# Strassen's seven products for Gate and Up of the last two token tiles in place of Down's

## The chip, the cores and the metric

One core of a Trainium2 chip runs the whole kernel. The metric is the device time of one execution in microseconds (us). The kernel before takes 804.02 us (median of 3 timed runs, 803.73 to 804.4). Engines are named as in the profile: PE (TensorE matmuls), PEld (its weight loads), DVE (VectorE), ACT (ScalarE), POOL (GpSimd), SP (the queue that issues most DMAs).

## What is computed

A layer norm of x (2048 tokens, 512 features) feeds two branches. One is sliding-window attention with 32 heads of 16 features and a window of 256, followed by a 512x512 projection; the other is a gated feed-forward with 1792 hidden features. The output is x + attention * silu(feed-forward).

```python
xn = _layernorm(x, axis=-1)
s = attention(xn, A_wqkv, A_wo)          # 32 heads of 16, window 256
gate = xn @ w1                            # 512 -> 1792
up = xn @ w3                              # 512 -> 1792
g = silu((silu(gate) * up) @ w2)          # 1792 -> 512
return x + s * g
```

Everything is float32 at the edges. Inside, each float32 operand is held as a float16 high part and a float16 low part, so that a product is three matmuls (high*high, low*high, high*low). All matmul weights are scaled by powers of two first.

## The kernel before

**Tiles.** The tokens stand in four tiles `t` of 512 (`NT`, `TW`). The hidden features stand in 14 blocks `f` of 128 (`FB`). For one `t` and `f`, `gate_up` (L1048) makes two pieces of 12 matmuls of 512 columns: Gate, then Up, each into a PSUM bank of its own (`bank`, L163, which hands out `m0` and `m1` in turn; there are only these two). ACT takes the tanh of Gate (L1074), DVE multiplies it with Gate (L1078) and with Up (L1083), and the result is split into a high and a low half for Down.

**Down** adds up the 14 blocks. For tiles 0 and 1, `down` (L1272) does it in four groups of blocks and four blocks of tokens: 336 matmuls of 512 columns (L1284). For tiles 2 and 3 Strassen's algorithm is used: `fold_weights` (L998) makes sums of w2's quarters once, during tile 1, and stores them in `dFold`; `fold_first` and `fold_second` (L1119, L1131) make the sums of the hidden activations on POOL; `fold_down_piece` (L1186) runs the seven products, 588 matmuls of 256 columns (L1202); ACT and DVE read them out (L1216, L1220), and `unfold` (L1226) adds the seven results to four blocks of output.

**Attention** is cut into 32 units (a tile, a group of 8 heads, half of it). In each unit `pass1` (L653) finds the row maxima of the next scores (PE L671, DVE L685) and `pass2` (L738) makes scores (PE L759), masks (DVE L766), exponentials (ACT L769) and the products with V (PE L787). The scores have two PSUM tiles of two banks (`pss`), the products with V one (`pso`).

**What sets the order.** PE's order is the order of the program text. A unit's attention comes in four or five batches; `spread` (L1508) puts pieces of dense work (Gate, Up, Down, projections, values, totals) between them by their cost in columns. `later(n, f)` (L144) puts work n steps on. For the other engines a scheduler chooses the order when the program is built, and then each engine runs its own list from front to back. Work that reads a PSUM bank is put forward there (`urgent`, L138). Slots in SBUF come from `take` and `give` (L113, L120).

**Ends.** `total` (L1316) multiplies the attention by `wo` and joins the branches. After the last attention unit the queue runs off what is left: in the kernel before the last Gate and Up, the last seven Down products, `unfold`, and the four totals.

Of the kernel before, what the change touches and what calls it, by code (L numbers as in the profile page):

```python
# [10 lines left out]
F32 = mybir.dt.float32  # L11
# [28 lines left out]
XS = 2.0**10  # L40
# [4 lines left out]
HS = 2.0**4  # L45
# [7 lines left out]
SLOTS = 54  # L53
ORDERED = {ENGINE.PE}
GROUPS = ((0, 4), (4, 8), (8, 11), (11, 14))
FOLDS = ((0, 4), (4, 7))
FOLD_AT = (0, 1, 3, 5, 7, 9, 11)
# [26 lines left out]
def tile_block(ctx: ExitStack, tc: tile.TileContext, x, wqkv, wo, w1, w3, w2, out):  # L84
# [17 lines left out]
    fpool = pool("fpool", 2)  # L102
    psm = pool("psm", 1, PSUM)
# [57 lines left out]
    open_bank = [0]  # L161

    def bank(shape, dtype=F32):  # L163

        open_bank[0] = b = 1 - open_bank[0]
        return psm.tile(shape, dtype, name=f"m{b}", tag=f"m{b}", bufs=1)
# [62 lines left out]
    dFold = dram.tile([len(KINDS), P, FB // 2, 2 * D], F16, name="dFold")  # L229
# [117 lines left out]

    WQ = {}
# [3 lines left out]
    def weights(name, w):  # L352
# [16 lines left out]
        def cut(apart=0):  # L369
            if name == "wo":  # L370

                made = [take(F16) for _ in range(NC)]
                hi, lo = ([m[:, k * D:(k + 1) * D] for m in made] for k in range(2))
            else:
                both = [const.tile([P, NC, D], F16, name=f"{name}{k}") for k in "hl"]
                hi, lo = ([b[:, c, :] for c in range(NC)] for b in both)
# [176 lines left out]
    def value(j, scores_bank=False):  # L553
# [4 lines left out]
        def part(half):  # L558
# [9 lines left out]
            if half:  # L568
                with urgent():
                    nc.scalar.activation(V[:, j % VB, 0:H * VW].rearrange("p (h w) -> p h w", w=VW)[:, :, 0:DH],  # L570
                                         pv.rearrange("p (h d) -> p h d", d=DH), AF.Copy, scale=sc["uv"])
        return opening([(6, lambda h=h: part(h)) for h in range(2)])
# [294 lines left out]
    sg_scale = const.tile([P, FB], F32, name="sgs")  # L867
    p13 = const.tile([P, FB], F32, name="p13")
# [16 lines left out]
    def measure(f, apart=0, until=8):  # L885
# [4 lines left out]
        def scale(s=None):  # L890
            pp = small.tile([P, 2, 2], F32, name="pp")
            pi = small.tile([P, 2, 2], F32, name="pi")
# [3 lines left out]
        def rest(pp, pi):  # L896
# [5 lines left out]
            def cut(i, k):  # L902
# [3 lines left out]
                split_pool(a[:, 0:D], a[:, D:], raws[i][k], pi[:, k, i:i + 1])  # L906
# [18 lines left out]
    def load_down(t, f):  # L925
        if t:
            WF[t, f][1] = b = take(F16)
# [5 lines left out]
    def measure_down(k, f):  # L933
# [21 lines left out]
        def rest(p2):  # L955
# [5 lines left out]
            if k:  # L961
                nc.vector.tensor_max(fold_q, fold_q, q)
            else:
                nc.vector.tensor_copy(fold_q, q)
# [16 lines left out]
            if f1 == FB:  # L981
                later(4, fold_scales)
        beside_scores(2, scale)

    fold_q = const.tile([P, 1], F32, name="fq")
    fold_down = const.tile([P, 1], F32, name="fd")
    fold_w = const.tile([P, FB], F32, name="fw")
    folded = []

    def fold_scales():  # L990

        folded.append(0)
        with tc.issue_after(lasts["emptied"].ins):
            nc.vector.tensor_scalar(fold_down, fold_q, 1.0 / (HS * WS), None, op0=ALU.mult)
            nc.vector.reciprocal(fold_q, fold_q)
            nc.vector.tensor_scalar(fold_w, p13, fold_q, WS, op0=ALU.mult, op1=ALU.mult)

    def fold_weights(j):  # L998

        cell = {}  # L1000
        l, r = slice(0, 256), slice(256, 512)
        sub = nc.gpsimd.tensor_sub

        def load():
            cell["raw"] = [take(F32) for _ in range(2)]
            for i, raw in enumerate(cell["raw"]):
                lasts["load"] = nc.sync.dma_start(raw, w2[(2 * j + i) * P:(2 * j + i + 1) * P, :])

        def sums():
            assert folded  # L1010
            e, o = cell["raw"]
            for i, raw in enumerate((e, o)):
                with behind_exp():
                    nc.scalar.activation(raw, raw, AF.Copy, scale=fold_w[:, 2 * j + i:2 * j + i + 1])
            cell["z"] = z, y = [take(F32) for _ in range(2)]
            sub(z[:, l], e[:, r], e[:, l])
            sub(z[:, r], o[:, r], z[:, l])
# [686 lines left out]
```

## Time and profile before

| what | value |
|---|---|
| median of 3 timed runs | 804.02 us (803.73 to 804.4) |
| span of the profiled execution, first to last instruction | 801.8 us |
| granted PE clock, mean | 1.000 |
| DVE busy | 623.0 us, 78% of the span |
| ACT busy, POOL busy | 393.9 us, 381.2 us |
| DMA engines' mean share, q1 | 55.4% |
| HBM read, written | 91.23 MB, 36.57 MB |

The profile has no other time of its own execution than the span; the timed runs lie 2.2 us above it, for what comes before the first and after the last instruction. A row of a group reads: line, engine, operation, tile written <- tiles read, shapes, count | busy us, mean ns of one | idle time ahead of it and whom it waited for. A row of the timeline reads: start, length, engine, line, operation, count. A row of the table by stage reads: stage, its length, then the busy time (and number of instructions) of PE, PEld, DVE, ACT and POOL, PE's granted clock, the DMA share and GB/s.

### The profile page before, as it was taken

The numbers are of one execution on the slowest core, as the hardware profiler recorded it, in microseconds if no ns is written. First come the engines' busy times: TensorE is split into PE (matmuls) and PEld (weight loads), VectorE is DVE, ScalarE is ACT, GpSimd is POOL, SyncE is SP. The second block draws the span as 40 slices with busy tenths as digits, with TensorE's granted clock in tenths as the row PEclk, the third lists the DMA queues.
The fourth block names the chain that finished last, engine by engine and source line by source line (L and its number), as shares of the span: only waits on it lengthen the run. The fifth ranks groups of instructions, "written<-read, shape, count | busy, mean of one in ns | idle before, by whom it ended". The sixth has DMA issues, their size and how long they took to land.

```text
span 801.8 us, 23974 instructions
## 1 busy us (share of the span) xinstructions
PE 791.1 (99%) x9181; PEld 403.8 (50%) x9181; DVE 623.0 (78%) x2005; ACT 393.9 (49%) x592; POOL 381.2 (48%) x746
## 2 busy tenths in 40 slices
PE   8999999999999999999999999999999999999997
PEld 4443445444454444444445444466544744466465
DVE  8887889778797778787888887776678876874537
ACT  6989777744355544344443344344434334444411
POOL 2355657633229435365442546330446276650770
PEclk9999999999999999999999999999999999999999
DMA  9987654636666565657555733665453553334431
GB/s 281 245 258 238 196 185 144 248 111 208 173 215 189 169 210 144 214 148 258 130 194 173 213 114 101 177 173 157 137 159 87 159 157 110 89 117 134 129 94 56
DMA packets 109858, 134.18 MB, mean 167 GB/s; under 512 B 18928, under 2 KB 64944, under 8 KB 109744
## 3 DMA queue, kind: packets, MB, share of 16 engines
q1 hardware_dynamic: 109456, 132.13, 55.4%
q8 instruction: 72, 1.18, 0.6%
q10 hardware_dynamic: 288, 0.52, 0.2%
q14 instruction: 42, 0.34, 0.1%
HBM read 91.23 MB, written 36.57 MB: 159 GB/s over the span
## 4 chain that ended last, share of the span: by engine, by line
PE 80%; DVE 8%; DMA 4%; ACT 3%; issue 2%; POOL 1%; SPq 1%; DVEq 0%; ACTq 0%; POOLq 0%
PE m L1059 31%; PE po L787 9%; PE m L601 8%; PE m L1202 8%; PE m L1284 7%; PE s L759 5%; PE m L1336 4%; PE m L567 4%; PE s L671 3%; DMA slot<-in_B_w_dram 2%; DVE junk L685 2%; PE po L671 2%; ACT sqa L249 1%; DVE s L766 1%; POOL slot L345 1%
## 5 line engine op out<-in xcount | busy, mean ns | idle before, releaser
L1059 PE MATMUL m<-XH,slot 128*128 128x512 f16 x896 | 267.3, 380 | 1.1 <-DVE slot L1078 0.6
L769 ACT ACTIVATE pt<-s,es 128x1024 f32<-128x1024 f32 x152 | 167.6, 1112 | 178.7 <-DVE s L766 176.9
L1059 PEld LDWEIGHTS <-slot 128*128 128x128 f16 x1344 | 124.9, 98 | 155.6 <-issue 13.1
L1059 PE MATMUL m<-XL,slot 128*128 128x512 f16 x448 | 169.8, 379 | 0.0
L766 DVE TENSOR_TENSOR s<-s,MK 128x256 f32<-128x256 f32 (+2 forms) x280 | 118.7, 434 | 53.5 <-PE s L759 49.8
L685 DVE CUSTOM_DVE_ANT_0 junk<-s,MW 128x320 bf16<-128x320 f32 x276 | 133.9, 485 | 18.4 <-PE s L671 11.4
L339 POOL TENSOR_TENSOR slot<-slot,slot 128x256 f16<-128x256 f32 (+1 forms) x86 | 57.6, 692 | 128.8 <-ACT slot L1092 60.0
L345 POOL TENSOR_TENSOR slot<-slot,slot 128x128 f16<-128x128 f32 x168 | 68.9, 444 | 76.6 <-ACT slot L343 76.6
L685 DVE CUSTOM_DVE_ANT_0 junk<-po,MW 128x320 bf16<-128x320 f32 x172 | 83.4, 485 | 4.6
L1284 PE MATMUL m<-slot,slot 128*128 128x512 f16 x336 | 78.5, 380 | 1.1 <-DVE slot L1078 1.1
L787 PE MATMUL po<-pt,V 64*32 64x320 f32 (+4 forms) x2880 | 77.2, 342 | 0.1
L601 PE MATMUL m<-XH,slot 128*128 128x512 f16 x240 | 70.8, 380 | 0.5 <-DVE slot L1078 0.5
L1202 PE MATMUL m<-slot,slot 128*128 128x256 f16 x588 | 68.4, 273 | 0.0
L1074 ACT ACTIVATE slot<-m,sgs 128x512 f32<-128x512 f32 x56 | 38.3, 684 | 59.8 <-PE m L1059 59.7
L1117 POOL TENSOR_TENSOR slot<-slot,slot 128x256 f16<-128x256 f32 x98 | 64.6, 671 | 1.1
L1202 PEld LDWEIGHTS <-slot 128*128 128x128 f16 x588 | 56.2, 98 | 11.5 <-issue 2.8
L787 PEld LDWEIGHTS po<-pt,V 64*32 64x32 f32 x2880 | 50.4, 106 | 22.4 <-issue 0.8
L1078 DVE SCALAR_TENSOR_TENSOR slot<-slot,m 128x512 f32<-128x512 f32 x56 | 38.3, 684 | 28.9 <-ACT slot L1074 26.7
L759 PE MATMUL s<-qa,KA 50*64 50x320 f16 (+3 forms) x1472 | 58.3, 259 | 0.0
L601 PEld LDWEIGHTS <-slot 128*128 128x128 f16 x392 | 36.5, 98 | 42.6 <-issue 1.7
L759 PEld LDWEIGHTS <-KA 50*64 50x64 f16 x1472 | 30.1, 105 | 51.7 <-issue 32.8
L1284 PEld LDWEIGHTS <-slot 128*128 128x128 f16 x336 | 30.7, 98 | 39.2 <-issue 4.7
(194 smaller groups left out, 1131.5 us busy)
## 6 DMA issues: line engine op xcount, KB each, us to landing
slot<-dW SPq DMA_DIRECT2D x98, 256.0 KB
slot<-in_B_w_dram SPq DMA_DIRECT2D x56, 256.0 KB
slot<-dFold SPq DMA_DIRECT2D x48, 256.0 KB
dW<-slot SPq DMA_DIRECT2D x42, 256.0 KB
slot<-in_A_x_dram SPq DMA_DIRECT2D x30, 256.0 KB
KA<-dK SPq DMA_DIRECT2D x24, 288.0 KB
slot<-dWQ SPq DMA_DIRECT2D x24, 256.0 KB
qa<-dQ SPq DMA_DIRECT2D x30, 192.0 KB
```

Of the source, the lines that this page charges most:

```text
L339: op(out[:, c], a[:, c], b[:, c])
L345: nc.gpsimd.tensor_sub(lo[:, c:c + P], raw[:, c:c + P], hi[:, c:c + P])
L601: nc.tensor.matmul(cell["pp"][:, cols[n]], w[:, (a * NC + c) * P:(a * NC + c + 1) * P], b[:, c, cols[n]], start=n == 0 and (c, i) == parts ...
L685: lasts["maximum"] = nc.vector.tensor_tensor_reduce(out=junk[:, :n], in0=s[:, r, :n], in1=mask, scale=1.0, scalar=NEG, op0=ALU.add, op1=AL ...
L759: nc.tensor.matmul(s[64 * h:64 * h + 64, r, o:o + 64 * n], ka[rows, 2 * p + a, 64 * (m + 4):64 * (m + 5)], qa[rows, 2 * p + a, 64 * (m + k ...
L766: nc.vector.tensor_add(v, v, MK[:, kind, of:of + n, :].unsqueeze(1).to_broadcast([P, 2 * len(which), n, 64]))
L769: lasts["exp"] = nc.scalar.activation(pt, s, AF.Exp, scale=es)
L787: nc.tensor.matmul(cell["po"][32 * i:32 * i + 32, h, 64 * (m + k):64 * (m + k + n)], V[64 * h:64 * h + 64, (4 * t + m // 2) % VB, hd * VW: ...
L1059: nc.tensor.matmul(cell[k], w[:, (a * NC + c) * P:(a * NC + c + 1) * P], b[:, c, :], start=c == 0 and i == 0, stop=c == NC - 1 and i == 2)
L1117: nc.gpsimd.tensor_sub(lo, view, hi)
L1202: nc.tensor.matmul(cell["ps"][:, c], made[:, f:f + P], wj[:, g:g + 256], start=j == j0 and c == 0 and n == 0, stop=j == j1 - 1 and n == 2, ...
L1284: nc.tensor.matmul(ps, hh[:, a * TW + b * P:a * TW + (b + 1) * P], w[:, c * D:(c + 1) * D], start=f == f0 and i == 0, stop=f == f1 - 1 and ...
```

## The change

Down of tiles 2 and 3 becomes what it is for tiles 0 and 1, so `fold_weights`, `fold_first`, `fold_second`, `fold_down_piece` and `unfold` go. Gate and Up of tiles 2 and 3 become `quad(t, j)`, which takes the blocks 2j and 2j+1 together: a 2x2 scheme over (even block, odd block) and (first half, second half of the 512 features that are added up) and two halves of the tokens. Each of the seven products has 12 matmuls of 256 columns: 6 for Gate and 6 for Up, side by side in one bank.

- `weight_sums(j)` makes four sums of quarters of w1 and w3 on DVE (L1070 to L1073 of the changed kernel), with a scaling and a cast on ACT and a subtraction on POOL, and stores them in `dSum`. It runs for five pairs during tile 1 and for two during tile 2 (`QUAD_AT`).
- `token_sums(t)` makes the sums of the tokens' quarters on DVE, once for each of the two tiles (`HALVES_AT`).
- Three of the seven products use w1 and w3 as they are (`QW` 0 to 2, read from `dW1`), four use the sums.
- A product is not added up with others at the end. Product 6 is accumulated onto product 1 in the same bank, 5 onto that, 3 onto that; 7 has a second bank, and 4 is accumulated onto it. Between two of them the bank is read out: `copied` on ACT (L1175), `added` on DVE (L1180). `bank` keeps the first bank aside meanwhile (`retained`), so that all dense pieces in between get the other one.
- tanh and the gating come in four pieces of 256 columns (`activated`, ACT L1193, DVE L1197 and L1198), then `halved` splits the result for Down.
- `arranged` fixes the order: products 1 and 2, product 6 followed by one longer piece (a projection, a value, a total or a Down piece), then 5 and 7, 3 and 4. `spread` keeps such pairs together and puts attention between them where its cost says so. `LATE` says how many groups of Down follow each pair.
- The weights of V move from fixed tiles to slots and are given back; there are 53 slots and five tiles for read-out products (`cpool`). Token scale and hidden scale are halved. Loads of the projections' weights and the preparation of a later token tile move by a few pieces.

```diff
-XS = 2.0**10
+XS = 2.0**9
-HS = 2.0**4
+HS = 2.0**3
+CS = 2.0**-21
-SLOTS = 54
+SLOTS = 53
+QUAD_FROM = 2
+LATE = (3, 3, 2, 2, 2, 2, 2)
+QUAD_AT = ((1, 4), (1, 6), (1, 8), (1, 10), (1, 12), (2, 0), (2, 2))
+HALVES_AT = {2: (1, 11), 3: (2, 5)}
...
+    retained = [None]
     def bank(shape, dtype=F32):
-        open_bank[0] = b = 1 - open_bank[0]
+        open_bank[0] = b = 1 - (open_bank[0] if retained[0] is None else retained[0])
...
+    def weight_sums(j):
...
+        def sums(k):
+            a, b = cell[k]
+            add(b[:, r], b[:, l], b[:, r])
+            sub(b[:, l], a[:, l], b[:, l])
+            sub(a[:, l], b[:, r], a[:, l])
+            sub(a[:, r], a[:, r], a[:, l])
...
+    def quad(t, j):
...
+        def product(ps, w, x, first):
+            for k in range(2):
+                for c in range(2):
+                    for n, (a, b) in enumerate(((0, 0), (1, 0), (0, 1))):
+                        nc.tensor.matmul(ps[:, 256 * k:256 * k + 256], w(k, a, c), x(b, c),
+                                         start=first and k == 0 and c == 0 and n == 0,
+                                         stop=k == 1 and c == 1 and n == 2, skip_group_check=True)
+        def copied(ps):
+            made = cpool.tile([P, 512], F32, name="copy")
+            with urgent():
+                lasts["exp"] = nc.scalar.activation(made, ps, AF.Copy, scale=CS)
+            return made
+        def added(ps, other):
+            with urgent():
+                lasts["emptied"] = nc.vector.scalar_tensor_tensor(other, ps, CS, other, op0=ALU.mult, op1=ALU.add)
+            return other
...
+        def p1():
+            assert turned[t] == 4
+            cell["a"] = bank([P, 512])
+            retained[0] = open_bank[0]
+            product(cell["a"], plain(0), tokens(0, 0), True)
+            give(QW[t, j, 0])
+            cell["p1"] = copied(cell["a"])
+        def p2():
+            ps = bank([P, 512])
+            product(ps, plain(1), tokens(1, 0), True)
+            give(QW[t, j, 1])
+            activated(e, 0, added(ps, cell["p1"]))
+        def p6():
+            product(cell["a"], summed_up(0, 0), token_sum(1, 256), False)
+            cell["u2"] = copied(cell["a"])
+        def p5():
+            product(cell["a"], summed_up(1, 256), token_sum(0, 0), False)
+            cell["v5"] = copied(cell["a"])
+        def p7():
+            cell["b"] = bank([P, 512])
+            product(cell["b"], summed_up(1, 0), token_sum(0, 256), True)
+            give(QW[t, j, 5], QW[t, j, 6])
+            activated(o, 1, added(cell["b"], cell["v5"]))
+        def p3():
+            product(cell["a"], summed_up(0, 256), tokens(1, 256), False)
+            give(QW[t, j, 3], QW[t, j, 4])
+            retained[0] = None
+            activated(e, 1, copied(cell["a"]))
+        def p4():
+            product(cell["b"], plain(2), token_sum(1, 0), False)
+            give(QW[t, j, 2])
+            if j == FB // 2 - 1:
+                give(*HALF[t])
+            activated(o, 0, added(cell["b"], cell["u2"]))
...
+    def arranged(beside, mine):
...
```

What the change does to the lists of the engines is seen at three places. The first is DVE early in tile 2 of the feed-forward. Before, right after the `CAST mt` of one attention unit, there stand row maxima (`ISA junk`), one gating product and the masks (`MK`):

```order
L717 CAST mt_7905<-s_7894 32x128
L685 ISA junk_7916,M_7803<-po_7911,MW_111 128x320
L685 ISA M_7803 128x1
L685 ISA junk_7918,M_7803<-po_7911,MW_111 128x320
L685 ISA M_7803 128x1
L1078 SCALAR_TENSOR_TENSOR slot13_7939<-slot13_7939,m1_7925 128x512
L766 TENSOR_TENSOR s_7949<-s_7949,MK_119 128x4x64
L766 TENSOR_TENSOR s_7949<-s_7949,MK_119 128x2x2x64
```

In the changed kernel, at the first pair of that tile, the end of a gating step is followed by the four sums of one weight, a projection's read-out (L634), and only then by the masks of two score tiles:

```order
L1198 TENSOR_TENSOR slot45_7573<-slot45_7573,copy_7553 128x256
L1070 TENSOR_TENSOR slot18_7385<-slot18_7385 128x256
L1071 TENSOR_TENSOR slot18_7385<-slot19_7384,slot18_7385 128x256
L1072 TENSOR_TENSOR slot19_7384<-slot18_7385,slot19_7384 128x256
L1073 TENSOR_TENSOR slot19_7384<-slot19_7384 128x256
L634 SCALAR_TENSOR_TENSOR slot5_7611<-m0_7595,slot5_7611 128x512
L778 TENSOR_TENSOR s_7630<-s_7630,MK_122 128x4x64
L778 TENSOR_TENSOR s_7647<-s_7647,MK_122 128x4x64
```

One gating product of 512 columns per block has become gating steps and weight sums of 256 columns, which stand in one list with the masks. The second place is ACT, in the same tile. Before, exponentials (`pt`) alternate with casts and with the tanh that reads Gate's bank:

```order
L1074 ACTIVATE slot20_7404<-m1_7311,sgs_155 128x512
L769 ACTIVATE pt_7420<-s_7410,es0_332 128x1024
L1092 CAST slot53_7450<-slot20_7404 128x512
L769 ACTIVATE pt_7472<-s_7461,es0_332 128x1024
L618 ACTIVATE slot22_7506<-m1_7454 128x512
```

In the changed kernel, in the third pair of that tile, two exponentials stand ahead of the copy of product 5 (`copy_8644`), a tanh and two scalings follow, then comes the copy of product 3 (`copy_8683`) from the same bank:

```order
L781 ACTIVATE pt_8581<-s_8566,es1_398 128x1024
L781 ACTIVATE pt_8598<-s_8583,es1_398 128x1024
L1175 ACTIVATE copy_8644<-m0_8448 128x512
L1066 ACTIVATE slot18_8384<-slot18_8384,inv_160 128x512
L1066 ACTIVATE slot6_8385<-slot6_8385,inv_160 128x512
L1193 ACTIVATE slot0_8665<-copy_8644,sga_159 128x256
L1175 ACTIVATE copy_8683<-m0_8448 128x512
```

So the next product in that bank has to wait for a copy that has two exponentials in front of it. The third place is PE. Before, where a Gate piece ends and the Up piece begins, the bank changes from `m1` to `m0`:

```order
L1059 MATMUL m1_7925<-XH_3741,slot19_7518 128x512
L1059 LDWEIGHTS slot19_7518
L1059 MATMUL m1_7925<-XL_3742,slot19_7518 128x512
L1059 LDWEIGHTS slot34_7519
L1059 MATMUL m0_7942<-XH_3741,slot34_7519 128x512
```

In the changed kernel, in the third pair of tile 3 (the tenth in all), product 6 ends (`slot40` holds its weights) and product 5 begins in the same bank `m0`, with nothing between them:

```order
L1168 LDWEIGHTS slot40_11891
L1168 MATMUL m0_12153<-slot21_10782,slot40_11891 128x256
L1168 LDWEIGHTS slot23_11924
L1168 MATMUL m0_12153<-slot28_10594,slot23_11924 128x256
L1168 LDWEIGHTS slot23_11924
```

This is the only place where two products in one bank follow each other directly; elsewhere at least product 2, 7, 3 or 4 or a longer piece stands between them. In the 14 pairs, products 5, 7, 3, 4 stand without attention between them five times (pairs 3, 5, 9, 11, 12), products 1, 2, 6 four times (pairs 1, 7, 13, 14), and a dense piece follows product 4 without attention in between four times (after pairs 6, 7, 8 and 10, counting in order of time).

525 lines of the change are left out of this document (271 added, 254 removed).

## The prediction

> **What bounds the kernel now.** I read the page's busy times and slices first, then who made PE wait, then the price of a matmul.
>
> ```profile
> span 801.8 us, 23974 instructions
> PE 791.1 (99%) x9181; PEld 403.8 (50%) x9181; DVE 623.0 (78%) x2005; ACT 393.9 (49%) x592; POOL 381.2 (48%) x746
> ...
> PE   8999999999999999999999999999999999999997
> ...
> DVE  8887889778797778787888887776678876874537
> ```
>
> PE is busy in every slice; DVE comes next, mostly at seven or eight tenths. A busy PE could still be a PE that stretches its matmuls, so the waits and the spacing matter more than the share.
>
> ```profile
> PE m L1284 <- DVE slot L1078: 1.1, 1, 1.1
> PE m L1562 <- DVE onesb L193: 1.0, 1, 1.0
> ...
> 773.26 13.92 PE L1202 MATMUL m<-slot,slot 128*128 128x256 f16 x126
> ...
> 787.01 5.34 PE L1336 MATMUL m<-slot,slot 128*128 128x512 f16 x24
> ...
> L1202 PE MATMUL m<-slot,slot 128*128 128x256 f16 x588 | 68.4, 273 | 0.0
> L1284 PE MATMUL m<-slot,slot 128*128 128x512 f16 x336 | 78.5, 380 | 1.1 <-DVE slot L1078 1.1
> ```
>
> The longest wait of PE in the whole run is 1.1 us, for DVE. The spacing follows from a run's length less the last matmul's own time: (13.92 - 0.273)/125 = 0.109 us for 256 columns, (5.34 - 0.380)/23 = 0.216 us for 512. A short matmul costs half a long one, and the kernel before is a sum of these prices: PE's instruction stream is the bound in all stages.
>
> **What PE has to do, counted.** Removed are Gate and Up of two tiles, 672 long matmuls, and 588 short ones of Down: 672 x 0.216 + 588 x 0.109 = 145.2 + 64.1 = 209.3 us. Added are 14 pairs x 7 products x 12 = 1176 short ones and 336 long ones of Down: 128.2 + 72.6 = 200.8 us. PE's floor falls by **8.5 us**; I use 8.3, since spacings rounded less give 0.1092 and 0.2157. Counted in the order of the built program, these numbers of rows are there, so that the change leaves its work undone is excluded. Everything else on PE stays.
>
> The Trainium skill speaks against the change here. Its page "TensorE: Matmul & The Clock Gate", section "Back-to-back issue gap", gives for a stream of weight loads and matmuls a sustained 81 ns at 128 columns and 131 ns at 512, which is not in proportion. An estimate by interpolation of that page is 98 ns at 256, and the sum would be 588 x 98 - 336 x 131 ns = 13.6 us longer instead of shorter. The trace does not agree: it shows 109 and 216 ns.
>
> **DVE in the crowded stretch.** The added DVE work is not spread evenly: weight sums, the layer norm of the last tile and the first three pairs meet between the 18th and the 22nd `CAST mt`, four attention units, before at 417.4 to 507.5 us.
>
> ```profile
> 417.40:507.50 90.10, 90.03 (x1174) 43.92 (x1173) 75.76 (x232) 35.61 (x48) 43.03 (x74) 1.00 0.54 154
> 207.20:237.20 30.00, 29.94 (x416) 15.20 (x406) 27.14 (x93) 11.84 (x16) 6.57 (x13) 1.00 0.67 196
> ...
> L1083 DVE SCALAR_TENSOR_TENSOR slot<-m,slot 128x512 f32<-128x512 f32 x56 | 38.5, 687 | 13.9 <-PE m L1059 13.6
> L1078 DVE SCALAR_TENSOR_TENSOR slot<-slot,m 128x512 f32<-128x512 f32 x56 | 38.3, 684 | 28.9 <-ACT slot L1074 26.7 <-DMA rb<-de 2.0
> L477 DVE TENSOR_SCALAR slot<-slot,mv,rs 128x512 f32<-128x512 f32 x16 | 9.5, 612 | 0.4 <-POOL rs L474 0.4
> L1220 DVE SCALAR_TENSOR_TENSOR slot<-m,fd,slot 128x512 f32<-128x512 f32 x14 | 10.5, 748 | 7.0 <-PE m L1202 6.8
> L1236 DVE TENSOR_TENSOR slot<-slot,slot 128x256 f32<-128x256 f32 x8 | 2.9, 414 | 0.0
> ...
> 789.89 0.75 DVE L1236 TENSOR_TENSOR slot<-slot,slot 128x256 f32<-128x256 f32 x2
> ```
>
> DVE is busy for 75.8 of 90.1 us there now, and at 27.1 of 30 us elsewhere PE still loses nothing. In the same four units of the changed kernel 14 gating products go (7 x 0.684 + 7 x 0.687 = 9.6 us). There come 10 read-outs with an addition (priced as L1220, 7.5), 26 gating steps, 24 weight sums and 4 token sums of 256 columns (54 x 0.414 = 22.4, as L1236) and 4 centrings that stood earlier before (4 x 0.612 = 2.4): 32.3 us. By whole durations DVE needs 75.8 + 22.7 = 98.5 us. But two L1236 in a row take 0.75 us, so the second starts 0.336 after the first: instructions overlap by 0.08. On 54 more instructions that is 4.3 us, which leaves 94.2. PE's own dense work in these units is 288 x 0.109 + 156 x 0.216 = 65.1 us against 64.8 before, so PE would need 90.4. DVE is **3.8 us** over, with 8.1 as the upper end and 0 as the lower, if a lag of DVE is absorbed by the second score tile. I take 3.8. In the other units the same count leaves DVE at some 0.8 to 0.97 of PE, once at 1.0.
>
> The Trainium skill bears on which end holds. "VectorE: DVE Perf Modes", section "The DRAIN you can't avoid", says that the next Vector instruction does not start until the pipe is empty; by that the surplus would be 8.1 us. The row of 0.75 us for two says otherwise, as does that page's own exception for instructions that nothing holds.
>
> **Handing over a bank.** New is that a product is accumulated onto a bank that has just been read out, so PE must wait for the reader. The trace has the parts.
>
> ```profile
> 621.73 0.41 PE L759 MATMUL s<-qa,KA 50*64 50x320 f16 x8
> ...
> 622.37 0.83 PE L1202 MATMUL m<-slot,slot 128*128 128x256 f16 x6
> ...
> 775.42 0.75 DVE L1220 SCALAR_TENSOR_TENSOR slot<-m,fd,slot 128x512 f32<-128x512 f32 x1 [1.27 <-PE m L1202]
> ...
> 791.77 0.74 DVE L1340 SCALAR_TENSOR_TENSOR slot<-m,us,slot 128x512 f32<-128x512 f32 x1
> ...
> 792.56 2.75 PE L1336 MATMUL m<-slot,slot 128*128 128x512 f16 x12 [0.20 <-DVE slot L1340]
> ...
> L1216 ACT ACTIVATE slot<-m,fd 128x512 f32<-128x512 f32 x14 | 9.6, 686 | 21.1 <-PE m L1202 16.0 <-issue 5.0
> L769 ACT ACTIVATE pt<-s,es 128x1024 f32<-128x1024 f32 x152 | 167.6, 1112 | 178.7 <-DVE s L766 176.9
> ```
>
> The run that starts at 773.26 has its first 18 matmuls issued by 773.26 + 18 x 0.109 = 775.23, and the reader starts at 775.42: 0.19 later. A copy takes 0.69, and PE starts 0.05 after a reader ends (792.51 to 792.56). So a bank is free again 0.93 us after its product. The cover is one short product, 12 x 0.109 = 1.31 us, at 13 tight places (products 5, 7, 3, 4 without attention between them five times, 1, 2, 6 four times, a piece directly after product 4 four times), and nothing at one (6 and 5 of the tenth pair). Elsewhere a long piece or attention stands between, the latter for 0.64 us or more (621.73 to 622.37). If ACT is free, the 13 cost nothing and the one costs 0.9. If an exponential of 1.11 has just begun, a tight place costs 0.93 + 1.11 - 1.31 = 0.73 and the one 2.0. The ends are 0.9 and 13 x 0.73 + 2.0 = 11.5 us. ACT is busy for 35.6 of 90.1 us, so most places find it free: I take **1.5 us**, nearer to the lower end.
>
> **What costs nothing, and under which cover.**
>
> ```profile
> L1074 ACT ACTIVATE slot<-m,sgs 128x512 f32<-128x512 f32 x56 | 38.3, 684 | 59.8 <-PE m L1059 59.7
> L1092 ACT CAST slot<-slot 128x512 f16<-128x512 f32 x28 | 17.2, 615 | 31.1 <-DVE slot L1083 31.1
> L1114 ACT CAST slot<-slot 128x256 f16<-128x256 f32 x42 | 15.6, 403 | 59.9 <-DVE slot L1083 59.9
> L1117 POOL TENSOR_TENSOR slot<-slot,slot 128x256 f16<-128x256 f32 x98 | 64.6, 671 | 1.1
> ```
>
> ACT gets 56 copies of 0.69, 56 tangents of half width (0.40, as L1114) and 64 more casts and 28 scalings of 0.6 to 0.7 for halves and sums; it loses 28 tangents of 0.68, the 42 casts of L1114 and the work on Down's sums. That is some 60 us more on 394, under 60% of the span. POOL loses the folds, L1117 and its like, some 110 us of 381. About 34 more transfers of 256 KB pass through SP's queue (190 become 224), all loads of weights asked for about one pair ahead, some 20 us; at a DMA share of 0.54 this is cover enough, and if it went, product 1 of a pair would wait. At the end, the chain from product 4 of the last pair through addition, tanh, two gating steps, cast (L1092) and POOL's two subtractions (L1117) is 0.75 + 0.40 + 0.83 + 0.62 + 1.34 us and some 0.5 of starts, 4.4 in all, beside four groups of Down of 9 matmuls, 36 x 0.216 = 7.8. If these were not there, PE would wait for all of it.
>
> **Sum.** 801.8 - 8.3 + 3.8 + 1.5 = 798.8 us of span. The timed median lies 2.2 above the span, so I predict **801.0 us**, 0.4% less. About 0.2% (1.6 us) is what a measurement of this kernel can tell from no change: below 802.4 is faster, above 805.6 slower.
>
> **Rivals.**
>
> *The floor is reached* (0.12). DVE's lag is absorbed and the copies are in time: 801.8 - 8.3 + 0.9 + 2.2 = 796.6 or a little less. For it: DVE at 90% costs PE nothing in 207.2 to 237.2. Against: nowhere does DVE run a whole unit at 100%.
>
> *DVE is the bound and eats the gain* (0.24). Each list is fixed, so a DVE that is fully loaded also stands idle behind a tanh or a copy. With the surplus of 8.1: 801.8 - 8.3 + 8.1 + 1.5 + 2.2 = 805.3. The wait of L1284 for L1078 is such a wait.
>
> *PE waits at the handed-over banks* (0.22, slower). ACT works through its list in order, and ACT's exponentials wait 176.9 us in total for DVE's masks. Where DVE is late, an exponential is late, and the copy behind it too. With every tight place paid in full: 801.8 - 8.3 + 3.8 + 11.5 + 2.2 = 811.0. It decides the sign from 8.3 - 3.8 + 1.6 = 6.1 us on, 0.44 us at each of 14 places. For it: in the third pair two exponentials stand right ahead of the copy of product 5. Against: the copies are put forward, and ACT is 60% idle.
>
> *A short product is not half a long one* (0.02, slower). If the weight load of 98 ns did not hide beneath 109, each of the 588 matmuls that PE has more than it would need at equal columns adds: 14 ns each undo 8.3 us, 25 ns give 801.0 + 14.7 = 815.7.
>
> ```profile
> L1202 PEld LDWEIGHTS <-slot 128*128 128x128 f16 x588 | 56.2, 98 | 11.5 <-issue 2.8
> ```
>
> Against it stands the row itself: at 98 ns each, 588 short matmuls already run at 109. The rule of "TensorE: Matmul & The Clock Gate" named above would make this rival the likeliest; no spacing in this trace follows it.
>
> **How the numbers follow.** The forecast has 0.40. Faster: 0.40 + 0.12 = 0.52. Same: DVE's case, 0.24. Slower: 0.22 + 0.02 = 0.24. The forecast's own range is 798.5 to 802.4. The range to hold 8 in 10 goes from the floor, 796, to the middle of the slower rival, 808: it leaves out some 0.05 below and 0.13 above.
>
> **What would show it.** Right: groups of 256 columns with 1176 matmuls at 0.109 apart, PE's waits of a few us more for ACT copies (L1175) and DVE additions (L1180), and DVE at or above 95% busy for the stretch of the first three pairs, with the only long waits of PE there. The floor would show as PE's waits unchanged. The slower rival would show as PE idle before product 3, 6 or 5 in most pairs, with ACT's L1175 as releaser, right behind an exponential. A loss after the last attention unit, in product 1 waiting for a DMA, or in tiles 0 and 1, where I see none, would make the prediction wrong.

## The result and the profile after

The changed kernel takes **850.57 us** (median of 4 runs, 849.07 to 851.98) against 803.88 us for the kernel before on the same chip: 1.058 times as long, with a 95% interval of 1.0565 to 1.0595. That is 49.6 us above the forecast and outside its range. First the page of the changed kernel, with the busy times and the slices:

```profile
span 848.5 us, 24657 instructions
...
PE 794.3 (94%) x9433; PEld 431.6 (51%) x9433; DVE 688.9 (81%) x2181; ACT 450.5 (53%) x692; POOL 277.3 (33%) x545
...
PE   9999999999999999899988987999999988997998
...
DVE  8878898887988788988999897679787877875655
```

PE is busy for about as long as before (794.3 against 791.1 us), but in a span that is 46.7 us longer. So PE stands still, most of all from the 17th slice (339 us) on; the additions for the sums of the weights run from 273 us on, the pairs from 429 us on. The next view lists PE's longest waits; each row reads: who waited, for whom, us in total, how often, the longest one.

```profile
PE m L1168 <- ACT copy L1175: 8.7, 8, 1.7
PE m L613 <- DVE slot L1342: 5.5, 2, 5.3
PE m L1286 <- ACT copy L1175: 4.3, 4, 1.2
PE s L683 <- DVE M L697: 3.9, 4, 1.3
PE s L683 <- ACT pt L781: 3.3, 6, 0.7
PE s L771 <- DVE M L697: 3.2, 4, 2.0
PE m L1168 <- DVE slot L1310: 2.8, 4, 1.3
```

Three kinds of wait are new: products and Down for the copies of a product (L1175), a projection for a read-out of the output (L1342), and scores for DVE's maxima (L697). The kernel before had no wait above 1.1 us. The table by stage shows where the time went. The stages are cut where PE turns the maxima of the 14th, 18th, 22nd and 32nd unit (L711 before, L723 after), first the kernel before, then the changed one. (The prediction's window of the second stage stood 2.6 us too early; DVE's busy time in it differs by 0.3 us.)

```profile
332.10:420.00 87.90, 87.86 (x1056) 41.12 (x1046) 73.25 (x225) 39.01 (x50) 40.96 (x76) 1.00 0.58 180
420.00:510.10 90.10, 90.03 (x1181) 43.92 (x1174) 75.46 (x230) 35.81 (x49) 41.77 (x71) 1.00 0.55 156
510.10:727.70 217.60, 217.41 (x2782) 120.51 (x2772) 162.43 (x513) 88.16 (x113) 102.89 (x174) 1.00 0.49 137
727.70:801.80 74.10, 69.66 (x681) 42.92 (x680) 38.65 (x75) 22.84 (x33) 29.79 (x51) 1.00 0.34 98
```

```profile
332.00:424.20 92.20, 87.77 (x1044) 40.60 (x1038) 81.26 (x253) 43.42 (x58) 30.66 (x51) 0.98 0.58 181
424.20:537.10 112.90, 95.01 (x1323) 59.36 (x1316) 98.08 (x284) 57.94 (x86) 38.41 (x62) 0.97 0.60 182
537.10:773.30 236.20, 218.11 (x2932) 135.76 (x2924) 188.49 (x594) 114.18 (x161) 51.10 (x81) 1.00 0.49 150
773.30:848.50 75.20, 69.03 (x662) 41.24 (x662) 43.53 (x80) 25.34 (x37) 14.29 (x22) 1.00 0.23 70
```

The stages grow by 4.3, 22.8, 18.6 and 1.1 us. In the second stage, the prediction's crowded stretch, and in the third, PE stands idle for 18 us each (112.90 - 95.01 and 236.20 - 218.11). DVE is busy for 87% and 80% of them: not full, though PE waits. Below, these are the first to the fourth stage.

Two places show how the waits come about. The timeline at products 5, 7 and 3 of the ninth pair (start, length, engine, line, operation; in brackets the idle time ahead and its releaser):

```profile
689.81 1.15 PE L1168 MATMUL m<-slot,slot 128*128 128x256 f16 x9
...
689.98 2.12 ACT L781 ACTIVATE pt<-s,es 128x1024 f32<-128x1024 f32 x2 [1.82 <-DVE s L778]
...
691.98 0.60 ACT L1175 ACTIVATE copy<-m 128x512 f32<-128x512 f32 x1
692.61 0.69 DVE L1180 SCALAR_TENSOR_TENSOR copy<-m,copy 128x512 f32<-128x512 f32 x1 [1.47 <-ACT copy L1175]
692.63 0.38 PE L1168 MATMUL m<-XH,slot 128*128 128x256 f16 x2 [1.68 <-ACT copy L1175]
```

The nine matmuls of product 7 at 689.81 show that product 5 is over. Its bank must be copied before product 3 adds to it. But in ACT's list two exponentials stand ahead of the copy. They waited 1.82 us for DVE's masks, and run for 2.12 us. The copy starts at 691.98, product 3 at 692.63, 1.68 us late. ACT was not short of time: it was idle until 689.98, with the copy behind an instruction that could not start. The second place is the longest wait:

```profile
522.62 1.47 SPq L1085 DMA_DIRECT2D dSum<-slot  x1
...
524.08 1.11 ACT L781 ACTIVATE pt<-s,es 128x1024 f32<-128x1024 f32 x1 [4.31 <-DVE s L778]
...
526.48 0.63 ACT L1332 ACTIVATE slot<-slot 128x512 f32<-128x512 f32 x1 [1.30 <-DMA dSum<-slot]
527.15 0.69 DVE L1333 SCALAR_TENSOR_TENSOR slot<-slot,slot 128x512 f32<-128x512 f32 x1 [2.17 <-ACT slot L1332]
527.87 0.75 DVE L1342 SCALAR_TENSOR_TENSOR slot<-m,us,slot 128x512 f32<-128x512 f32 x1
...
528.68 1.01 PE L613 MATMUL m<-XH,slot 128*128 128x512 f16 x2 [5.32 <-DVE slot L1342]
```

Read from the bottom: a projection waits 5.32 us for a bank, the bank for DVE's read-out L1342, this for DVE's L1333 ahead of it, this for ACT's tanh L1332, and the tanh for its output buffer: that SBUF slot still held a sum of the weights whose store to `dSum` was on its way. The store alone accounts for the last 1.30 us of it: until 525.19 ACT had another instruction ahead of the tanh in its list, an exponential that had itself waited 4.31 us for a mask. A stored buffer and ACT's fixed order together thus stopped DVE and PE.

### The profile page after: what moved, and what is told of

The parts are those of the page before. It is cut to its first block, busy times and chain, and to the rows that moved or that the text cites. A ratio compares the mean times of both kernels' runs of the same rounds, so it can differ in the third digit from the quotient of the medians.

```text
span 848.5 us, 24657 instructions
## 1 busy us (share of the span) xinstructions
PE 794.3 (94%) x9433; PEld 431.6 (51%) x9433; DVE 688.9 (81%) x2181; ACT 450.5 (53%) x692; POOL 277.3 (33%) x545
## 5 line engine op out<-in xcount | busy, mean ns | idle before, releaser
L344 POOL TENSOR_TENSOR slot<-slot,slot 128x256 f16<-128x256 f32 (+1 forms) x208 | 140.8, 702 | 410.9 <-ACT slot L1250 153.0
L1286 PE MATMUL m<-slot,slot 128*128 128x512 f16 x672 | 156.2, 382 | 6.3 <-ACT copy L1175 4.3
L697 DVE CUSTOM_DVE_ANT_0 junk<-s,MW 128x320 bf16<-128x320 f32 x276 | 133.4, 483 | 9.3 <-PE s L683 2.4
L1014 PE MATMUL m<-XH,slot 128*128 128x512 f16 x448 | 133.7, 380 | 1.3 <-DVE slot L1342 0.8
L1168 PEld LDWEIGHTS <-slot 128*128 128x128 f16 x1176 | 111.8, 98 | 38.7 <-issue 22.8
L1286 PEld LDWEIGHTS <-slot 128*128 128x128 f16 x672 | 62.3, 98 | 83.8 <-issue 14.7
L1014 PEld LDWEIGHTS <-slot 128*128 128x128 f16 x672 | 62.4, 98 | 78.9 <-issue 7.8
L697 DVE CUSTOM_DVE_ANT_0 junk<-po,MW 128x320 bf16<-128x320 f32 x172 | 83.4, 485 | 3.7
L1168 PE MATMUL m<-slot,slot 128*128 128x256 f16 x672 | 80.6, 273 | 5.7 <-ACT copy L1175 3.4
L1014 PE MATMUL m<-XL,slot 128*128 128x512 f16 x224 | 84.9, 379 | 0.0
L613 PE MATMUL m<-XH,slot 128*128 128x512 f16 x240 | 72.6, 388 | 7.4 <-DVE slot L1342 5.5
L1168 PE MATMUL m<-XH,slot 128*128 128x256 f16 x336 | 57.0, 273 | 9.3 <-ACT copy L1175 5.3
L613 PEld LDWEIGHTS <-slot 128*128 128x128 f16 x392 | 37.3, 99 | 51.4 <-issue 12.5
L799 PEld LDWEIGHTS po<-pt,V 64*32 64x32 f32 x2880 | 51.1, 106 | 22.4 <-issue 1.7
L360 POOL TENSOR_TENSOR slot<-slot,slot 128x128 f16<-128x128 f32 x112 | 46.7, 452 | 47.8 <-ACT slot L357 47.7
L683 PE MATMUL s<-KA,qa 48*64 48x320 f16 (+3 forms) x824 | 45.6, 295 | 9.3 <-DVE M L697 3.9
L1180 DVE SCALAR_TENSOR_TENSOR copy<-m,copy 128x512 f32<-128x512 f32 x42 | 28.9, 687 | 29.7 <-PE m L1168 16.6
```

What stands on the lines that cost most here:

```text
L344: op(out[:, c], a[:, c], b[:, c])
L360: nc.gpsimd.tensor_sub(lo[:, c // 2, at], raw[:, c * P:(c + 1) * P], hi[:, c // 2, at])
L613: nc.tensor.matmul(cell["pp"][:, cols[n]], w[:, (a * NC + c) * P:(a * NC + c + 1) * P], b[:, c, cols[n]], start=n == 0 and (c, i) == parts ...
L683: nc.tensor.matmul(s[c:c + w, r, :n], qa[rows, 2 * p + a, ii * P + c:ii * P + c + w], ka[rows, 2 * p + a, e - n:e], start=True, stop=True)
L697: lasts["maximum"] = nc.vector.tensor_tensor_reduce(out=junk[:, :n], in0=s[:, r, :n], in1=mask, scale=1.0, scalar=NEG, op0=ALU.add, op1=AL ...
L799: nc.tensor.matmul(cell["po"][32 * i:32 * i + 32, h, 64 * (m + k):64 * (m + k + n)], V[64 * h:64 * h + 64, (4 * t + m // 2) % VB, hd * VW: ...
```

## The experiments

Three theories follow. **1, slots:** the 53 slots run short while the sums are made, and engines wait for stores. **2, DVE:** its new additions and gating steps, and what waits behind them in its fixed list. **3, banks:** products wait for copies that stand behind exponentials. The changed kernel's four runs lie within 0.35% of each other; the kernel before took 803.7 to 804.6 us beside the experiments. Differences are taken from 850.57. Each of e1 to e14 is one run, so a difference of less than some 2 us says little; e15 has four runs. The edits are shown shortened.

### What giving up the folded Down costs (e1)

```diff
-QUAD_FROM = 2
+QUAD_FROM = 4      # no pairs, no sums: all tiles with gate_up and down (and Down's loads)
-QUAD_AT = ((1, 4), ...)   HALVES_AT = {2: (1, 11), 3: (2, 5)}
+QUAD_AT = ()              HALVES_AT = {}
```

> Gate, Up and Down of all four token tiles with long matmuls, no Strassen at all: what giving up the kernel before's short Down costs by itself. PE has 1008 long matmuls in tiles 2 and 3 where the kernel before has 672 long and 588 short ones: 217.4 - 209.2 = 8.3 us more. If the loss of the changed kernel lies in what was added (buffers, DVE, banks), this kernel takes 803.9 + 8 = 812 us, within 3. If giving up the folded Down itself did the harm (its removal moved other work), it takes 825 us or more.

Measured: 816.11 us, 4 above PE's sum. Of the 12 us above the kernel before, 8.3 are PE's longer program. Giving up the folded Down did little more, so the harm of the change is in what it adds. PE is busy for 800.3 us there, against 791.1 + 8.3 = 799.4 by the prices.

### Leaving the sums of the weights out (e2), DVE's additions alone (e3)

```diff
 def work():                      # e2: weight_sums makes nothing
+    return
-    nc.sync.dma_start(made, dSum[(i - 3) // 2, (i - 3) % 2, j])
+    nc.sync.dma_start(made, dW1[2 * j + (i - 3) // 2, (i - 3) % 2])

 def sums(k):                     # e3, in weight_sums and in token_sums
+    return
```

> The sums of the Gate and Up weights are left out altogether (no loads, scalings, additions, casts or stores of them; the products that would use them load the plain weights instead), so the values are not the reference's. PE's work is unchanged. Theory 1 (slots run short between the 342nd and 413th step and ACT, DVE and SP wait for transfers and POOL) and theory 2 (DVE and its fixed order in the stretch) both take the excess of the units from the 15th to the 22nd (5.0 + 22.7 us) away: 850.6 - (20 to 28) = 823 to 831 us. Theory 3 (banks handed over from copy to product) keeps the loss: 843 to 850.

> Only DVE's additions and subtractions that form the sums of weights and of token columns are left out (56 + 16 of 256 columns, about 30 us of DVE); loads, scalings, casts, stores and buffers stay, the values are not the reference's. Theory 2 (DVE's load and order): as without weight sums, 823 to 833 us. Theory 1 (slots): the waits stay, 843 to 850 us. Theory 3 (banks): 845 to 850.

Measured: 834.98 us without the sums (15.6 less), 841.27 without DVE's additions (9.3 less). The stages of e2, first to third:

```profile
331.80:419.70 87.90, 86.04 (x1036) 40.27 (x1032) 75.33 (x236) 34.30 (x41) 20.16 (x35) 1.00 0.49 136
419.70:522.00 102.30, 93.33 (x1328) 58.89 (x1322) 84.68 (x260) 45.17 (x63) 21.80 (x38) 0.98 0.43 126
522.00:757.90 235.90, 218.00 (x2928) 135.65 (x2920) 188.54 (x593) 114.16 (x161) 51.10 (x81) 1.00 0.50 150
```

The sums cost 4.3 us in the first stage and 10.6 in the second, and nothing in the third, as they should. Both runs fall short of what theory 2 expected: more than half of the stretch's loss and all of the third stage's stay.

### Copies that do not read the bank (e4)

```diff
-nc.scalar.activation(made, ps, AF.Copy, scale=CS)
+nc.scalar.activation(made as [128, 4, 128], identf four times, AF.Copy, scale=CS)
```

> ACT's copies of products 1, 6, 5 and 3 read a constant tile in SBUF instead of the bank (same work, wrong values), so no product waits for a copy and no copy for a product. Theory 3 (handing over): PE's waits for copies (13.5 us by the profile) go, and with them most of the steady 2 us a unit from the 23rd unit on: 825 to 832 us, the excess of the stretch staying. Theories 1 and 2: the waits only move to other places, 838 to 848 us.

Measured: 844.79 us, 5.8 less. The total lies in the range of theories 1 and 2; but the third stage takes 225.60 us instead of 236.20, 10.6 less, which is in keeping with theory 3. The first stage became 7.9 us longer, though it has no product yet. Copies that wait for no product also move in the lists: the first of them runs at 8.3 us, in the changed kernel at 432.1. So this run is no clean measure of the whole.

### When a slot counts as free (e5)

```diff
 weight_sums, token_sums, halved: POOL reads, then
-    give(raw, after=20)
+    give(raw, after=6)
 weight_sums: store to dSum, then
-    give(made, after=10)
+    give(made, after=25)
```

> Only the numbers change by which a slot counts as free again: the buffers read by POOL's subtractions after 6 steps instead of 20, the stored sums of the weights after 25 instead of 10. Slots taken before they are due fall from 75 of 1812 requests in three passes (25 a pass, up to 16 steps early) to 23 a pass, at most 11 early, and fewer of them still under a store. Theory 1 (slots) in full: the wait of 5.3 us in the 22nd unit and the halved clock behind it go and some of the 15th unit's loss: 850.6 - (7 to 14) = 837 to 844 us. If slots matter only at that one place: 842 to 847. Theories 2 and 3: 848 to 852.

Measured: 843.17 us, 7.4 less, as theory 1 expected. Which engine computes what is the same; a buffer that POOL has read is taken again sooner, one that is being stored later. The second stage shrinks from 112.90 to 106.30, the clock in it is not halved any more, and no projection waits for L1342 any more (a wait of 0.8 us of a Gate or Up piece for it is left, as in the changed kernel):

```profile
424.50:530.80 106.30, 92.70 (x1324) 58.72 (x1316) 97.18 (x282) 57.69 (x86) 38.35 (x62) 1.00 0.62 185
```

The order changed too: the same tanh (L1332) now runs at 520.00, ahead of the exponential, which starts at 526.70. Up to the end of the first stage (424.5 against 424.2 us) nothing is won, since ahead of that stage Down waits 3.1 us for a gating product (L1038), a wait that the changed kernel doesn't have.

### Gating (e6), all three causes off (e7), one tile alone (e8)

```diff
 def gated():                     # e6
-    nc.vector.scalar_tensor_tensor(h, h, 1.0, made[:, 0:256], op0=ALU.add, op1=ALU.mult)
-    nc.vector.tensor_mul(h, h, made[:, 256:512])
+    pass
 e7: the edits of e2, e4 and e6 together
 e8: QUAD_FROM = 3, HALVES_AT = {3: (2, 11)}; tile 2 as in e1
```

> DVE's 112 gating steps of 256 columns are left out (46 us of DVE; ACT's casts take the tangent alone, so the values are wrong). Theory 2, with the chain of addition, tangent and gating in DVE's fixed order: 23.6 us are lost from the 23rd unit on, 11.6 of which the copies did not take; these and half of the stretch go: 850.6 - (17 to 25) = 826 to 834 us. Theory 3 alone (banks): only the copies count, DVE's load does not: 843 to 850.

> No sums of weights, copies that read SBUF, and no gating steps, all at once; the values are wrong, PE's program is unchanged. If the three are the whole loss, this is the floor: 803.9 - 8.3 = 795.6 us, and up to 4 more for read-outs by DVE: 796 to 800. If some of the loss sits in PE itself (short products, retained banks) or in loads for the pairs, it stays at 808 us or more.

> Strassen on Gate and Up of the fourth tile only; the third tile with long matmuls, as in the kernel without Strassen (816.1). PE's floor is 8.3 below that one: 807.8. If a pair costs 2 to 2.5 us wherever it stands (banks and DVE's chain), the units from the 26th on keep their 17 us and the sums come with some 5: 825 to 832 us. If the loss is mainly the meeting of sums, layer norm and first pairs: 809 to 816 us.

Measured: 844.10 us without gating, 6.5 less. The third stage gives 5.7 back (230.50), the second 3.2 (109.70); the second begins 2.6 us later. Theory 2 expected 17 or more. With all three off 810.65 us: 39.9 of the 46.7 us are gone, and the third stage takes 219.30. The remaining 15 us above the floor of 795.6 are not named by these three. With the last tile alone 823.13 us: 15 above its floor for seven pairs, between the 825 that I gave for a cost per pair and the 816 of the rival. The first three stages of e8 show that both have a part:

```profile
333.40:422.50 89.10, 88.24 (x1052) 41.52 (x1048) 75.64 (x240) 42.25 (x56) 27.90 (x50) 1.00 0.63 193
422.50:515.00 92.50, 90.68 (x1180) 44.01 (x1172) 82.52 (x251) 48.20 (x65) 35.32 (x54) 1.00 0.61 187
515.00:745.70 230.70, 220.02 (x2798) 123.13 (x2786) 183.24 (x570) 104.09 (x138) 50.50 (x81) 1.00 0.46 138
```

PE is idle for 10.7 us of the third stage, where the seven pairs stand, so pairs cost time away from the sums. But e8 makes all the sums of the weights too, with DVE's additions between 269 and 484 us, and PE is idle for only 0.9 and 1.8 us in the first two stages. So the sums cost PE next to nothing where no pair, and nothing that belongs to a pair, stands beside them; what e2 won is their meeting with these.

### Attention between the products (e9)

```diff
 in spread(), between two attention batches:
+    if not first and hasattr(dense[0][0][1], "apart"):
+        break
     at += c
-    run(dense.pop(0))
+    first = first and not c
+    last = dense.pop(0)
+    run(last)
+    if hasattr(last[-1][1], "ends"):
+        break
 in quad():
+    for i in (2, 3, 5):           # products 6, 5 and 3
+        pieces[i][1].apart = True
+    pieces[6][1].ends = True      # product 4
```

> The order of PE's pieces alone changes: between two attention batches at most one of the runs 1-2, 6, 5-7, 3-4 of a pair, and no other piece right behind product 4. 11 of the 14 places where a product or piece follows its bank's last product with one product or none between get attention in between. By the profile PE waits 16.5 us at these 14 places. Theory 3 (copies late behind exponentials, no cover): 10 to 14 us go: 837 to 841 us. If ACT and DVE are simply late everywhere and the wait only moves to the scores: 847 to 851 us.

Measured: 834.52 us, **16.1 less**, more than expected. No work is left out: only PE's order changes. PE's waits, and the second and third stage:

```profile
PE s L683 <- ACT pt L781: 6.3, 15, 0.7
PE m L613 <- DVE slot L1345: 4.5, 1, 4.5
...
PE m L1168 <- ACT copy L1175: 1.6, 2, 0.9
```

```profile
423.60:532.60 109.00, 95.30 (x1330) 60.11 (x1322) 94.86 (x284) 57.57 (x86) 39.53 (x62) 0.97 0.63 188
532.60:758.70 226.10, 218.29 (x2930) 138.08 (x2924) 190.44 (x590) 112.02 (x158) 52.22 (x78) 1.00 0.55 157
```

The waits for copies fall from 13.0 us (8.7 + 4.3) to 1.6, and scores wait 3.0 us more for exponentials. The third stage gives 10.1 us back, the second 3.9. The copies are as many and as long as before; they only have attention for cover now. DVE's load in the third stage is the same (190.44 against 188.49), so it was not less work for DVE that helped there. The slot's wait (L1345 here) is still there, as it should.

### Additivity (e10), later gating (e11)

```diff
 e10: the edits of e3 and e5 together
 e11, in activated():
-    later(3, gated)
+    later(5, gated)              # and the casts behind it at 6 and 7
```

> DVE's additions for the sums left out (values wrong) and slots given by use, together. If DVE's additions (9.3 us) and the slots (7.4 us) are two separate losses, they add up to what leaving the sums out altogether gave (15.6 us): 832 to 836 us. If both runs removed the same delay: 839 to 843 us.

> The two gating steps and the casts behind them are asked for two steps later, nothing else. DVE waits 11.6 us for tangents by the profile, with masks and maxima queued behind. If the loss from gating (5 to 7 us) is this waiting in a fixed order: 843 to 847 us. If it is the 46 us of DVE work itself: 849 to 852 us.

Measured: 833.83 and 852.43 us. DVE's additions (9.3) and the slots (7.4) add up to the 16.7 of e10, close to the 15.6 of leaving the sums out: two losses, which together are about what the sums cost. Asking for the gating later gained nothing. But in e11 DVE still waits for tangents as long as before:

```profile
DVE slot L1197 <- ACT slot L1193: 12.1, 20, 1.2
```

The edit did not take the wait away, so this run doesn't tell whether gating costs by its work or by its waiting. That stays open.

### Repairs (e12 to e15)

```diff
 e12: the edits of e9 and e5, and in weight_sums and token_sums
-    add, sub = nc.vector.tensor_add, nc.vector.tensor_sub
+    add, sub = nc.gpsimd.tensor_add, nc.gpsimd.tensor_sub
 e13: e12 with the edit of e6        e14: e12 with the edit of e2
 e15: e12, and in weight_sums
-    later(n + 14 + 2 * i, lambda i=i, k=k: cut(i, k))
+    later(n + 20 + 2 * i, lambda i=i, k=k: cut(i, k))
```

> Attention between the products, slots given by use, and the additions of the sums on POOL instead of DVE (88 x 0.67 = 59 us on POOL, which was busy for a third of the span). If the three losses are separate: 850.6 - 12 - 7.4 - (5 to 9) = 822 to 826 us. If POOL's additions hold its other subtractions and the slots up: 830 us or more. By the floor of all three taken away (810.7) it doesn't reach the kernel before.

> The three repairs (822.5 us) with DVE's 112 gating steps left out (values wrong). Without the repairs leaving them out gave 6.5 us. If gating is a loss of its own: 815 to 817 us. If it only cost because copies and slots were late: 820 to 823 us. If DVE's load is now the bound of the rest: 806 to 812 us.

> The three repairs (822.5 us) with the sums of the weights left out altogether (values wrong). If the repairs took all that the sums cost: 820 to 823 us. If the sums' transfers, scalings and casts still cost in the 19th to 22nd unit (14.2 us above the kernel before there): 812 to 818 us.

> The three repairs, and ACT's casts of the weight sums are asked for 6 steps later, since ACT waited 15.1 us for POOL's additions by the profile of the three repairs. If that waiting in ACT's fixed order cost PE time: 816 to 820 us. If it cost nothing, or the slots held 6 steps longer take it back: 821 to 825 us.

Measured: 822.49 us with the three repairs, as expected. That is 28.1 less, where e9, e5 and e3 one by one make 32.8; POOL does the additions now, which e3 left out. In e12 ACT's casts (L1079) waited for POOL's additions (L1073):

```profile
ACT slot L1079 <- POOL slot L1073: 17.1, 7, 4.2
```

With the casts later e15 takes 820.15 us (819.89 to 821.13), 2.3 less than the one run of e12, which is too little to call this wait a loss of its own. It is the best version with right values here and still 1.0199 times as long as the kernel before (1.0182 to 1.0216). On top of e12, leaving out gating gives 4.8 us (817.73, between the first two ranges) and leaving out the weight sums 6.9 (815.60: their transfers, scalings and casts still cost). The stages of e15, second and third:

```profile
418.80:519.70 100.90, 92.04 (x1328) 58.85 (x1318) 87.50 (x256) 57.23 (x86) 58.09 (x90) 1.00 0.65 199
519.70:745.10 225.40, 217.96 (x2926) 137.87 (x2918) 184.60 (x578) 112.09 (x158) 59.72 (x90) 1.00 0.52 158
```

PE is idle for 8.9 and 7.4 us there, against 17.9 and 18.1 in the changed kernel. No version tried beats the kernel before; even without the sums of the weights, copies from the bank and gating (e7) the time is still 810.65.

## Why the prediction was wrong

PE's shorter program came out as forecast, but what was put on top of it was far too small: 1.5 us for the banks, 3.8 for DVE, and nothing for the slots or for gating outside the stretch. The paths that were missed run through the fixed lists of ACT and DVE.

**The floor was right.** The nine short matmuls at 689.81 above are (1.15 - 0.273)/8 = 0.1096 us apart, as forecast. With the waits mostly gone (e7) PE is busy for 785.9 us; the forecast was 791.1 - 8.3 = 782.8. The rival by which a short product is not half a long one is out, and with it the rule that would have made it likely, of the Trainium skill's page "TensorE: Matmul & The Clock Gate", section "Back-to-back issue gap". PE's program did get shorter, but PE stood idle for 43.5 us more (848.5 - 794.3 against 801.8 - 791.1). Its busy time, 794.3, is 11.5 above the forecast 782.8 as well. An estimate puts 4.3 of these down to the halved clock, half of the 3.40 and 5.28 us in the table of the last section; and each pause counts the 0.273 us of the matmul ahead of it in full, where 0.109 is counted in a stream.

**The handover of a bank was the right mechanism at the right places, with a price ten times too small.** Forecast were 14 places and 1.5 us. PE's list shows waits for copies at 12 places, 13.0 us, and taking the places apart gave 16.1 (e9). Two steps failed. "ACT is busy for 35.6 of 90.1 us, so most places find it free" read a busy share as if a free engine were a ready one; ACT's list waits for masks, in the changed kernel as before:

```profile
ACT pt L781 <- DVE s L778: 198.9, 104, 8.1
```

An ACT that is idle behind a mask is not free for the copy. And "with every tight place paid in full", 0.73 us each, counted one exponential that has just begun, where the ninth pair has two that haven't. The rival of PE waiting at the banks had the right sign, and its 11.5 us were too few.

**DVE in the crowded stretch: the instructions were counted right, the time wrong.** Forecast were 98.5 us by whole durations and, after 4.3 off for overlap, 94.2 for the stage; DVE is busy for 98.08, in 112.90 us. That 98.08 is near 98.5 is in part luck: the gating steps and the sums take 26.5 us of the stage, not 22.4, since they run slower than 0.414, and the sums of one weight start 0.46 us apart, without overlap:

```profile
L1198 DVE TENSOR_TENSOR slot<-slot,copy 128x256 f32<-128x256 f32 x13 | 6.9, 528 | 0.0
L1073 DVE TENSOR_TENSOR slot<-slot 128x256 f32<-128x256 f32 x6 | 3.3, 542 | 0.0
...
510.74 0.42 DVE L1070 TENSOR_TENSOR slot<-slot 128x256 f32<-128x256 f32 x1 [0.28 <-ACT slot L1066]
511.20 0.42 DVE L1071 TENSOR_TENSOR slot<-slot,slot 128x256 f32<-128x256 f32 x1
511.66 0.42 DVE L1072 TENSOR_TENSOR slot<-slot,slot 128x256 f32<-128x256 f32 x1
```

The larger step that failed is the assumption that a loaded DVE works without a break, so that its new work would first fill its idle time. DVE is idle for 14.8 us of the stage, as it was before (90.10 - 75.46 = 14.6), and the new work came on top. Leaving out the sums gives 10.6 us of the stage back, attention between the products 3.9, leaving out gating 3.2.

**The slots were not in the sum at all.** The diff takes one slot of 54 away and adds sums that occupy them; I asked of no transfer whose buffer it holds. That is 7.4 us (e5), 6.6 of them in the second stage, with the wait of 5.32 us and the halved clock behind it; the transfer there was itself costed at nothing.

**What was costed at nothing.** ACT got 56.6 us more (450.5 - 393.9; forecast some 60), POOL lost 104 (forecast 110), and the tail grew by 1.1 us and shrinks to 74.0 in e9: these hold. The gating steps were priced only in the stretch. They are slower than forecast (0.414), and DVE has 11.6 us of idle time for the tangents ahead of them:

```profile
L1197 DVE SCALAR_TENSOR_TENSOR slot<-slot,copy 128x256 f32<-128x256 f32 x56 | 25.1, 450 | 11.6 <-ACT slot L1193 11.6
L1198 DVE TENSOR_TENSOR slot<-slot,copy 128x256 f32<-128x256 f32 x56 | 27.0, 482 | 0.7
```

Leaving them out gives 6.5 us, 5.7 of them in the third stage, where the forecast had DVE at 0.8 to 0.97 of PE and no cost. "Tiles 0 and 1, where I see none" was named as what would make the prediction wrong: the first stage lost 4.3 us there. Without the sums of the weights it takes 87.90 as before (e2), but e8 with these sums takes 89.10; what e8 lacks there are the token sums and the loads for the pairs of tile 2, so the sums seem to cost this only beside these.

**The account.** Banks 16.1 (e9), sums of the weights 15.6 (e2; slots 7.4 and additions 9.3 make 16.7), gating 6.5 (e6): 38.2 of the 55 us that lie between the floor of 795.6 and 850.57, if they add up, which the three repairs did only in part. e7, which takes these causes away in another way, leaves 15 us. e1, which has no pairs at all, also lies 4 above its own sum; whether these are the same 4 is not shown. What the other 11 are is open. About half of it lies in the second stage, where PE is still idle for 6.0 of 97.50 us in e7, in many waits of at most 1.7 us.

## What to carry to other kernels

An engine with a fixed list is available when the instruction ahead of yours can start, not when it is idle: before putting a read-out behind PE, look at what stands ahead of it in its list, and what that waits for. Count the cover of a reused bank against that whole queue, and put other work of PE in between, which was worth 16.1 us here, net of the scores' longer waits. Where a change adds stored or loaded intermediates, follow each buffer to the transfer that frees it, since the next user may be on the critical path of another stage. And see what such intermediates meet: the same sums of the weights cost PE next to nothing in e8, where no pair stood beside them.

## What the runs showed of the hardware

A wait of PE costs more than its own length when the clock drops behind it. The stages around the two drops in the changed kernel (the last figures are clock, DMA share and GB/s):

```profile
343.20:346.60 3.40, 3.40 (x23) 1.43 (x23) 3.40 (x11) 2.39 (x4) 0.00 (x0) 0.50 0.09 31
527.50:534.30 6.80, 5.28 (x12) 1.76 (x12) 4.18 (x10) 0.31 (x1) 1.41 (x2) 0.50 0.16 52
```

The granted clock is 0.50 for 3.4 us and for 6.8 us, and the matmuls of 512 columns in it are 0.43 us apart (529.48 and 529.91) instead of 0.216. The second drop begins within the wait of 5.32 us that began at 523.4, and PE works at half speed for 5.6 us after it. The first follows a wait of only 2.0 us, for maxima that stood in DVE's list behind a sum of the tokens:

```profile
339.16 1.68 DVE L344 TENSOR_TENSOR slot<-XH,XL 128x256 f32<-128x256 f16 x2 [1.54 <-POOL slot L344]
...
342.38 0.42 PE L771 MATMUL s<-qa,KA 50*64 50x320 f16 x12 [2.02 <-DVE M L697]
```

The Trainium skill, "TensorE: Matmul & The Clock Gate", section "Why this matters for your kernels", advises to leave no idle gap of PE above about 3 us. The second drop agrees; the first shows that 2 us can do, with 0.4 us more right behind, and in e2 the clock is 0.50 from about 515 to 518 us after a single wait of 1.54 us that ended at 514.08. Length alone does not decide: after the changed kernel's waits of 1.7 and 1.8 us elsewhere there is no drop. In e15 the mean clock is 0.999, with no drop before the last 4 us.
